# A fused attention and mixture-of-experts kernel: seven expert weight blocks split during the attention, the last head's first half gated two steps sooner, and the written order held through expert 0's first tile

## The chip, the core and the metric

The kernel runs on one core of one Trainium2 chip. The metric is device microseconds (us) of one execution. The engines are named as the profile names them: PE is the matrix engine (PEld its weight loads), DVE the vector engine, ACT the scalar engine, POOL the GpSimd engine, SP the engine whose queue issues most of the DMA transfers. Each engine works through its own instructions in the order in which they stand, and they meet at semaphores.

## What is computed

Two batches of eight heads of attention over 768 positions, in which a query sees only the keys of its own cluster, and then a mixture of eight experts over the 1536 resulting rows, each row sent to its best expert:

```python
mask = q_assign[:, :, :, None] == k_assign[:, :, None, :]
scores = scale * np.matmul(q, k.transpose(0, 1, 3, 2))
scores = np.where(mask, scores, -1000000000.0)
...
attn = attn / (np.sum(attn, axis=-1, keepdims=True) + 1e-09)
return np.matmul(attn, v).astype(np.float32)
...
logits = x @ w_gate
expert_idx = np.argmax(logits, axis=1)
...
h = np.maximum(np.einsum('ecd,edf->ecf', disp, w1), 0.0)
y = np.einsum('ecf,efd->ecd', h, w2)
...
        out[i] = gate_w[i] * y[expert_idx[i], pos[i]]
```

`w1` is 8 x 512 x 1024 and `w2` is 8 x 1024 x 512; an expert keeps its first 384 rows.

## The kernel before

**The attention.** Sixteen heads (index `i` or `h`, 0 to 15; heads 0 to 7 are batch 0) go one after the other. A head has twelve groups `g` (0 to 11). Group `g` is `st_group`: two matmuls (L395, L396) that make a 128 x 384 piece `s` of the scores in PSUM (three buffers), and one ACT instruction (L400) that writes its exponentials to `pf`. What else happens in a group stands in `hooks(i, g)`, called behind each `st_group`; so the order on every engine is written out by hand, and where `held[0]` is set, `keep` pins PE, DVE and ACT instructions to it. The row maxima of a later head are made ahead (`max_tile`, matmuls `m` on PE, reductions `mx` on DVE); they end in head 14's group 2.

At group 2 of head `i` the second half of head `i-1` is finished: `pv_batch` (12 matmuls `o<-pf,v`), sums of the exponentials by matmuls with ones (`sum_strips`, `rsp`), and their copies out of PSUM by ACT (`rs`, `oT`). At groups 5 and 6 the sums are turned (`sum_turn`, `rtp<-cs,rs`, into the one buffer of the PSUM pool `psO` that the values `o` also use) and inverted on DVE (`r`). `out_stage` makes output and gate logits at once (`otp<-rhb,oT`), `out_scale` scales them on DVE into `lg` (logits) and `x`.

**The last head** (15) goes through its keys for the first half of the queries in groups 0 to 5, for the second half in groups 6 to 11. `last_batch` makes values and sums of one half, `sum_turn`, `last_rows` and `last_scale` finish it. Before, the first half starts at group 8, the second after group 11.

**The gate** (`gate`) of three or six row tiles: on DVE the maximum logit (`gmx`), a one-hot row (`goh`) and, from counts that PE makes (`gps`), each row's place (`gsi`); softmax weight by `gex` and `gsm` into `x`. Then POOL scatters each row tile to the table `xd` in DRAM (L649, one indirect DMA a tile, six for the last head). Row tiles of expert 0 beyond the first are read back from `xd` (L806, `row`) and so wait for all six. Expert 0's first tile of 128 rows (tile 0) is full from batch 0 and lies in `row0` since head 10.

**The weights** come in 64 blocks of 512 KB, eight for each expert (0 to 3 of `w1`, 4 to 7 of `w2`). SP loads a block to one of four raw buffers (`wraw`), ACT copies its high part to `ws` (L131, `w_high`), DVE subtracts to get the low part (L137, `w_split`). A raw buffer is free again, and the load of the block four later is issued on SP, when DVE has split it. `W_AT` names the groups in which blocks are split during the attention: before, blocks 0 to 3, as only four `ws` places exist until the attention's tiles (pool `stat`) are freed by `sta.close()` in `moe`. Blocks 4 to 7 are split in expert 0.

**Expert 0** is done tile by tile by `single`: turn the rows (`turn`: four transposes on PE, high part by ACT, low part by DVE: `xha`, `xla` for tile 0, `xhc`, `xlc` for tile 1), two column halves of 12 matmuls each (L878) with ReLU by ACT (`hf`), each turned in the same way (`hha`, `hla`; `hhc`, `hlc`), then 24 matmuls (L848). Between its pieces stand the rest of the last head (`tail`), the row loads, and the splits of expert 0's second four blocks and of expert 1's first four (blocks 8 to 11). Experts 1 to 7 follow, each 448 matmul instructions of L909 and L910 in all seven, with their blocks split on the way.

Of the kernel before, what the change touches and what calls it, by code (L numbers as in the profile page):

```python
# [7 lines left out]
F32 = mybir.dt.float32  # L8
# [15 lines left out]
def kernel(  # L24
# [35 lines left out]
    W_AT = [(13, 8), (14, 2), (14, 8), (15, 2)]  # L60
# [28 lines left out]
    att, sta = ctx.enter_context(ExitStack()), ctx.enter_context(ExitStack())  # L89
    stat = sta.enter_context(tc.tile_pool(name="stat", bufs=1))  # L90
    work = att.enter_context(tc.tile_pool(name="work", bufs=2, side="right"))
    rhb = work.tile([P, H, 2 * OW], F32, name="rhb", bufs=1)
# [368 lines left out]
    def last_batch(h, j):  # L461
        o, ps = psO.tile([P, 512], F32, tag="o", name="o"), psT.tile([P, 512], F32, tag="t", name="rsp")
        pf, a = pt.pop((h, j)), acc.pop((h, j))
        for n in range(TH):
            for c in range(2):
                keep(nc.tensor.matmul(
                    out=o[c * D:(c + 1) * D, 0:HALF],
                    lhsT=vt[h // 2][:, h % 2, 2 * n + c, :],
                    rhs=pf[:, n, c],
                    start=(n == 0),  # L470
                    stop=(n == TH - 1),
                ))
# [23 lines left out]

    def last_scale(h, j):
        b, hh = divmod(h, H)
        r = rt_t[h, "s"]
        tv = oT_t.pop(h)[:, 0:TH * OW].rearrange("p (c o) -> p c o", c=TH)  # L500
        ts = slice(j * TH, (j + 1) * TH)
        lt = work.tile([P, 2, TH, E], F32, tag="lt", name="lt")[:, 0]
        lg = xt[b, "l"][:, ts]
        keep(nc.vector.tensor_tensor(out=lt, in0=tv[:, :, D:OW], in1=r.to_broadcast([P, TH, E]), op=ALU.mult))
        keep(nc.vector.tensor_tensor(out=lg, in0=lg, in1=lt, op=ALU.add))
        keep(nc.vector.tensor_tensor(
            out=xt[b][:, ts, hh * D:(hh + 1) * D], in0=tv[:, :, 0:D], in1=r.to_broadcast([P, TH, D]), op=ALU.mult
# [47 lines left out]
    def gate(b, t0=0, t1=NT):  # L555
# [8 lines left out]
        keep(nc.vector.tensor_reduce(out=mx, in_=lg, axis=AX.X, op=ALU.max))  # L564
        eq = tl("geq")
# [26 lines left out]
        ex = tl("gex")  # L592
        keep(nc.vector.tensor_tensor(out=ex, in0=lg, in1=mx.to_broadcast(sh), op=ALU.subtract))
        keep(nc.scalar.activation(out=ex, in_=ex, func=AF.Exp))

# [78 lines left out]
    row0 = []  # L674

# [4 lines left out]
    def hooks(i, g):  # L680
        even, pi = i % 2 == 0, i // 2
        if g in (3, 9) and 2 <= i < 6:
            zero_fill(2 * (i - 2) + g // 6)
        if i == 3 and g == 0:
# [34 lines left out]
        if i > 0 and g == (G_B0 - 1 if i == NH - 1 else G_OUT) and i != H + 1:  # L719
# [3 lines left out]
        if (i, g) == (H + 1, 5):  # L723
            next(gens["g"])
        if g == G_B1 and i > 0:
# [20 lines left out]
        if g == (G_B0 if i else 2 * NT - 1):  # L746
            if i == NH - 1:
                p_add(i, 0)
                last_batch(i, 0)
            else:  # L750
                pv_batch(i, 0)
                p_add(i, 0)
# [5 lines left out]
            if i == NH - 1:  # L758
                out_scale(i - 1)
# [3 lines left out]
            if not even and i < NH - 3:  # L763
                for _ in gens["c"]:
                    pass
        if (i, g) in W_AT:
# [3 lines left out]
        if g == G_B0 + 1 and 0 < i < NH - 3:  # L770
# [506 lines left out]
```

## Time and profile before

| | us |
|---|---|
| three runs | 469.14, 473.61, 473.76; median 473.61 |
| the profiled execution | 472.46 |
| its span in the trace | 470.3 |
| busy in the span: PE / PEld | 444.9 (95%) / 346.0 (74%) |
| DVE / ACT / POOL | 321.4 (68%) / 272.7 (58%) / 138.5 (29%) |

Times in the rows below are counted from the start of the span. The attention ends at about 265 us; expert 0 ends and expert 1 starts at 299.48 us; the last matmul is over before 465 us. A busy matmul row is as long as the engine holds it, and neighbours overlap, so how long work takes is read from the starts: twelve matmuls of 512 columns start 2.82 us apart from the next piece, 0.235 us each.

### The profile page before, as it was taken

To read this page: it belongs to the slowest core of one execution; us is meant where nothing else is said; L and a number is where in the kernel's file an instruction comes from. 1 tells how busy PE (TensorE), PEld (TensorE's weight loads), DVE (VectorE), ACT (ScalarE), POOL (GpSimd) and SP (SyncE) were. 2 spreads that over 40 slices of the span, in tenths; PEclk is the share of its full clock that TensorE was granted. 3 is DMA by queue.
4 is the path that set the end of the run, shared out by engine and by line. 5 is a ranking of instruction groups with operands and counts; after the bars stand their busy time and mean duration, and the time that the engine had idled before them with its cause. 6 is when DMAs were issued, how large, how long until landed. Compare 5 with 4: busy or idle time off the path is not lost. (4 is left out here: it accounts for less than half of the span.)

```text
span 470.3 us, 8149 instructions
## 1 busy us (share of the span) xinstructions
PE 444.9 (95%) x2832; PEld 346.0 (74%) x2832; DVE 321.4 (68%) x682; ACT 272.7 (58%) x548; POOL 138.5 (29%) x168
## 2 busy tenths in 40 slices
PE   8899999999999989999999978999999999999984
PEld 7764766576666656667755556899999999899963
DVE  6785868678686795787754565587867777687411
ACT  4752655565666555566564624577786868586430
POOL 6793345736334356433000130001010101011010
PEclk9998999999999999999999999999999999999998
DMA  8366449976341514423112058659697878865110
GB/s 281 87 172 214 148 94 344 340 220 231 85 118 35 161 50 147 130 45 88 42 50 91 17 203 307 206 175 289 234 276 252 252 259 238 260 212 204 37 36 18
DMA packets 31223, 78.14 MB, mean 166 GB/s; under 512 B 4678, under 2 KB 5024, under 8 KB 31172
## 3 DMA queue, kind: packets, MB, share of 16 engines
q1 hardware_dynamic: 26340, 61.33, 43.4%
q0 software_dynamic: 4832, 16.15, 8.9%
q8 instruction: 30, 0.49, 0.4%
q14 instruction: 21, 0.17, 0.1%
HBM read 50.46 MB, written 16.76 MB: 143 GB/s over the span
## 5 line engine op out<-in xcount | busy, mean ns | idle before, releaser
L342 DVE TENSOR_REDUCE mx<-m 128x1 f32<-128x384 f32 x192 | 102.5, 553 | 54.1 <-PE m L335 52.2
L400 ACT ACTIVATE pf<-s 128x384 f32<-128x384 f32 x192 | 90.6, 492 | 54.8 <-PE s L396 49.9
L137 DVE TENSOR_TENSOR ws<-wraw,ws 128x1024 fp32r<-128x1024 f32 x64 | 78.1, 1223 | 32.2 <-ACT ws L131 32.0
L395 PE MATMUL s<-W,Y 112*128 112x384 f32 (+1 forms) x192 | 73.7, 384 | 2.0 <-ACT pf L400 2.0
L335 PE MATMUL m<-Y,W 112*128 112x384 f32 (+1 forms) x192 | 68.6, 361 | 5.0 <-DVE mx L342 3.1
L909 PE MATMUL g<-xc,ws 128*128 128x416 f32 x224 | 70.0, 373 | 1.2 <-PEq L1046 0.3
L131 ACT ACTIVATE ws<-wraw 128x1024 fp32r<-128x1024 f32 x64 | 67.0, 1050 | 4.5 <-DMA wraw<-in_w_dram 4.5
L909 PE MATMUL g<-hc,ws 128*128 128x416 f32 x224 | 69.5, 371 | 0.0
L649 POOL DMA_INDIRECT out_dram<-y,row x17 | 18.0, 1057 | 171.5 <-ACT pt L917 110.9
L415 PE MATMUL o<-pf,v 128*64 128x384 f32 x360 | 66.2, 496 | 0.4 <-DVE r L457 0.4
L396 PE MATMUL s<-Qs,Y 97*128 97x384 f32 (+1 forms) x192 | 65.7, 342 | 0.4 <-issue 0.3
L910 PE MATMUL g<-xc,ws 128*128 128x208 f32 x224 | 58.1, 259 | 1.0 <-issue 1.0
L910 PE MATMUL g<-hc,ws 128*128 128x208 f32 x224 | 57.9, 259 | 0.0
L298 POOL TENSOR_TENSOR ql<-qv,W 64x256 fp32r<-64x256 f32 x45 | 39.9, 912 | 51.3 <-ACT W L311 26.2
L298 POOL TENSOR_TENSOR Y<-kv,Y 64x256 fp32r<-64x256 f32 x48 | 41.4, 889 | 43.3 <-ACT Y L316 42.0
L395 PEld LDWEIGHTS s<-W,Y 112*128 112x128 f32 (+1 forms) x192 | 36.5, 190 | 23.2 <-issue 16.6
L917 ACT ACTIVATE pt<-g 128x208 f32<-128x208 f32 x84 | 27.5, 340 | 32.0 <-PE g L910 27.9
L335 PEld LDWEIGHTS m<-Y,W 112*128 112x128 f32 (+1 forms) x192 | 36.5, 191 | 12.9 <-DVE mx L342 8.1
L909 PEld LDWEIGHTS g<-xc,ws 128*128 128x128 f32 x224 | 42.1, 188 | 3.3 <-issue 2.9
L415 PEld LDWEIGHTS o<-pf,v 128*64 128x64 f32 x360 | 23.4, 137 | 28.3 <-issue 24.8
L910 PEld LDWEIGHTS g<-xc,ws 128*128 128x128 f32 x224 | 42.8, 191 | 1.2 <-issue 1.2
L910 PEld LDWEIGHTS g<-hc,ws 128*128 128x128 f32 x224 | 42.7, 191 | 0.0
(206 smaller groups left out, 700.6 us busy)
## 6 DMA issues: line engine op xcount, KB each, us to landing
wraw<-in_w_dram SPq DMA_DIRECT2D x64, 512.0 KB
xd<-z POOLq DMA_DIRECT2D x7, 780.0 KB
row<-xd SPq DMA_DIRECT2D x18, 260.0 KB
qv<-in_qT_dram SPq DMA_DIRECT2D x8, 384.0 KB
kv<-in_kT_dram SPq DMA_DIRECT2D x8, 384.0 KB
v<-in_v_dram SPq DMA_DIRECT2D x8, 384.0 KB
Y<-Y SPq DMA_DIRECT2D x32, 96.0 KB
Qs<-W SPq DMA_DIRECT2D x16, 192.0 KB
```

Of the source, the lines that this page charges most:

```text
L131: keep(nc.scalar.activation(out=w[:, 0], in_=raw[c], func=AF.Copy))
L137: keep(nc.vector.tensor_tensor(out=w[:, 1], in0=t, in1=w[:, 0].bitcast(F32), op=ALU.subtract))
L298: keep(eng.tensor_tensor(out=out[:, cc], in0=a[:, cc], in1=b[:, cc].bitcast(F32), op=ALU.subtract))
L335: keep(nc.tensor.matmul(out=m[:, 0:HALF], lhsT=W[0:KA[h % 2], t * P:(t + 1) * P], rhs=Y1[0:KA[h % 2], j * HALF:(j + 1) * HALF], start=True ...
L342: keep(nc.vector.tensor_reduce(out=mxt[h][:, j, t:t + 1], in_=m[:, 0:HALF], axis=AX.X, op=ALU.max))
L395: keep(nc.tensor.matmul(out=s[:, 0:HALF], lhsT=Y1[0:ka, ks], rhs=W[0:ka, qs], start=True, stop=False))
L396: keep(nc.tensor.matmul(out=s[:, 0:HALF], lhsT=Y0[0:kb, ks], rhs=Qs[0:kb, qs], start=False, stop=True))
L400: keep(nc.scalar.activation(out=pt[h, u][:, slot[0], slot[1]], in_=s[:, 0:HALF], func=AF.Exp, scale=1.0 / float(D) ** 0.5))
L415: keep(nc.tensor.matmul(out=ot[h][j * D:(j + 1) * D, 0:HALF], lhsT=vt[h // 2][:, h % 2, kt, :], rhs=pf[:, n, j], start=(kt == 0), stop=(kt ...
L909: nc.tensor.matmul(out=o, lhsT=w[0], rhs=x.rearrange("p o n -> p (o n)"), start=start, stop=False)
L910: nc.tensor.matmul(out=o[:, 0:RW], lhsT=w[1], rhs=x[:, 0], start=False, stop=stop)
L917: nc.scalar.activation(out=t, in_=o[:, RW:2 * RW], func=AF.Copy)
```

## The change

1. Seven blocks (0 to 6) are split in the attention instead of four: at groups (12,8), (13,2), (13,8), (14,2), (14,8), (15,2), (15,6). The persistent tiles of the heads with an even pair (12 and 13 are the last of them) stand in a pool of their own that is closed at the start of head 14; its room takes the three new `ws` places. The fourth, for block 7, is split behind the last scores. In the groups of `W_AT` the ACT copy is issued ahead of the rest of the group's work.
2. The last head's first half is started at group 6 instead of 8, and its logits and the first half of the gate are done inside groups 10 and 11. The second half's sums come ahead of its values. In `gate` the softmax weight (`gex`, `gsm`) is done sooner, also for batch 0 in head 9.
3. The order stays pinned through the end of the gate: `tail` becomes a generator, three of whose steps stand at named matmuls of expert 0's first tile, and `turn` and the first products are kept in order too.
4. Expert 0 splits only block 7 and then expert 1's blocks 8 to 11.

```diff
-    W_AT = [(13, 8), (14, 2), (14, 8), (15, 2)]
+    W_AT = [(12, 8), (13, 2), (13, 8), (14, 2), (14, 8), (15, 2), (15, 6)]
+    NW = len(W_AT)
...
-        return [[stat.tile([P, S], dt, name=f"{nm}{par}{j}") for j in range(2)] for par in range(2)]
+        return [[stat[j].tile([P, S], dt, name=f"{nm}{par}{j}") for j in range(2)] for par in range(2)]
...
+        if not sums_first:
+            values()
         for q in range(4):
             keep(nc.tensor.matmul(
...
+        if sums_first:
+            values()
...
         keep(nc.vector.tensor_reduce(out=mx, in_=lg, axis=AX.X, op=ALU.max))
+        ex = tl("gex")
+        keep(nc.vector.tensor_tensor(out=ex, in0=lg, in1=mx.to_broadcast(sh), op=ALU.subtract))
+        keep(nc.scalar.activation(out=ex, in_=ex, func=AF.Exp))
         eq = tl("geq")
...
+        sm = tl("gsm", 1)
+        keep(nc.vector.tensor_reduce(out=sm, in_=ex, axis=AX.X, op=ALU.add))
+        keep(nc.vector.tensor_scalar(out=sm, in0=sm, scalar1=1e-9, scalar2=None, op0=ALU.add))
+        keep(nc.vector.reciprocal(out=xt[b][:, t0:t1, DM:DM + 1], in_=sm))
         v, w = tl("gv"), tl("gw")
...
+        if (i, g) == (NH - 2, 0):
+            sta.close()
+            wslot.append(ctx.enter_context(tc.tile_pool(name="wsl", bufs=1, reuse_waits="tile")))
+            for c in range(NA, NW):
+                slots.append(wslot[0].tile([P, 2, 1024], R32, name=f"ws{c}"))
...
-        if i > 0 and g == (G_B0 - 1 if i == NH - 1 else G_OUT) and i != H + 1:
+        if i > 0 and g == (6 if i == NH - 1 else G_OUT) and i != H + 1:
             out_stage(i - 1)
...
+        if (i, g) in W_AT:
+            w_high(W_AT.index((i, g)))
         if g == G_B1 and i > 0:
             pv_batch(i - 1, 1)
...
+        if i == NH - 1:
+            if g == 5:
+                keep(nc.vector.tensor_tensor(out=rhl, in0=rhb[:, H - 1, 0:OW], in1=rhb[:, H - 1, OW:2 * OW], op=ALU.add))
+                p_add(i, 0)
+            if g == 6:
+                last_batch(i, 0)
+                sum_evict(i)
+                pv_evict(i)
+            if g == 7:
+                out_scale(i - 1)
+            if g == 8:
+                sum_turn(i)
+            if g == 9:
+                last_rows(i, 0)
+            if g == 10:
+                last_logits(i, 0)
+                gens["g"] = gate(B - 1, 0, TH)
+                next(gens["g"])
+            if g == 11:
+                next(gens["g"])
+                p_add(i, 1)
+                last_scale(i, 0)
...
-                next(a)
-                tail()
-                for _ in range(FF // 512):
-                    next(a)
-                more_slots(NA)
-                for c in range(NA, 2 * NA):
+                def tail_step():
+                    next(tail, None)
+
+                a = single(0, 0, "a", both, {(0, 0, 0): tail_step, (0, 0, 2): tail_step, (0, 3, 1): tail_step})
+                b = single(0, 1, "b", both)
+                next(a)
+                tail_step()
+                next(a)
+                next(a)
+                more_slots(2 * NA - NW)
+                for c in range(NW, 2 * NA):
                     w_high(c)
...
-                for _ in range(2):
+                for _ in range(2 * NA - NW):
                     w_next()
                 next(a)
-                for _ in range(2):
-                    w_next()
                 next(a)
...
+        def rest():
+            next(gens["g"])
+            yield
+            for _ in gens["g"]:
+                pass
+            last_batch(h, 1, True)
+            sum_evict(h)
+            pv_evict(h)
+            sum_turn(h)
+            yield
+            last_rows(h, 1)
+            last_logits(h, 1)
+            g = gate(B - 1, TH, NT)
+            next(g)
+            next(g)
+            last_scale(h, 1)
+            yield
+            for _ in g:
+                pass
+            counts()
+            held[0] = False
```

**Place 1, ACT, head 14's first groups.** `pf` are exponentials, `rs` and `oT` the copies of head 13's sums and values, `ws` a block's high part. Before:

```order
L400 ACTIVATE pf_2871<-s_2868 128x384
L400 ACTIVATE pf_2871<-s_2876 128x384
L400 ACTIVATE pf_2871<-s_2883 128x384
L443 ACTIVATE rs_2913<-rsp_2904 128x384
L425 ACTIVATE oT_2915<-o_2830 128x384
L131 ACTIVATE ws1_112<-wraw_912 128x1024
L400 ACTIVATE pf_2871<-s_2921 128x384
```

Of the change:

```order
L402 ACTIVATE pf_2882<-s_2879 128x384
L402 ACTIVATE pf_2882<-s_2894 128x384
L402 ACTIVATE pf_2882<-s_2901 128x384
L133 ACTIVATE ws3_117<-wraw_919 128x1024
L445 ACTIVATE rs_2932<-rsp_2923 128x384
L427 ACTIVATE oT_2934<-o_2842 128x384
L402 ACTIVATE pf_2882<-s_2939 128x384
```

The block's copy (block 3 now, block 1 before) moved from behind the two copies to ahead of them; in head 15 the same holds for block 5.

**Place 2, PE and DVE, the end of the last head.** On PE, `s` are score pieces, `rtp<-cs,rs` turned sums, `otp` output and logits, `rtp<-cs,row0` the turned rows of expert 0's first tile, `gps` the gate's counts, `g1` expert 0's products. PE before, from the turn of the first half's sums on:

```order
L450 MATMUL rtp_3100<-cs_75,rs_3092 128x128 x3
L395 MATMUL s_3104<-W11_97,Y111_101 128x384
L396 MATMUL s_3104<-Qs11_105,Y011_109 128x384
L493 MATMUL otp_3112<-rhl_93,oT_3094 128x72 x3
L466 MATMUL o_3131<-pf_3050,v_2641 64x384 x6
L474 MATMUL rsp_3132<-acc_3120,onef_85 32x384 x2
L474 MATMUL rsp_3132<-pf_3050,onef_85 32x384 x2
L878 MATMUL g1_3261<-ws0_111,xha_3186 128x512 x2
L584 LDWEIGHTS trib_81
L584 MATMUL gps_3147<-goh_3129,trib_81 128x48
```

PE of the change, from the same turn on, and then from the last of the counts on:

```order
L452 MATMUL rtp_3114<-cs_75,rs_3098 128x128 x3
L397 MATMUL s_3118<-W11_100,Y111_104 128x384
L398 MATMUL s_3118<-Qs11_108,Y011_112 128x384
L502 MATMUL otp_3126<-rhl_96,oT_3100 128x72 x3
L397 MATMUL s_3130<-W11_100,Y111_104 128x384
L398 MATMUL s_3130<-Qs11_108,Y011_112 128x384
L397 MATMUL s_3147<-W11_100,Y111_104 128x384
L398 MATMUL s_3147<-Qs11_108,Y011_112 128x384
L843 MATMUL rtp_3165<-cs_75,row0_2365 128x128 x4
L602 LDWEIGHTS trib_81
L602 MATMUL gps_3172<-goh_3151,trib_81 128x48
```

```order
L608 MATMUL gps_3172<-gcum_2169,oneb_82 128x48
L481 MATMUL rsp_3205<-acc_3153,onef_85 32x384 x2
L481 MATMUL rsp_3205<-pf_3071,onef_85 32x384 x2
L470 MATMUL o_3204<-pf_3071,v_2644 64x384 x6
L452 MATMUL rtp_3220<-cs_75,rs_3216 128x128 x3
L909 MATMUL g1_3187<-ws0_114,xha_3161 128x512 x2
L502 MATMUL otp_3230<-rhl_96,oT_3218 128x72 x3
```

DVE of the change at that place (`acc` adds the second half's exponentials for `rsp_3205`, `x_2328` are the first half's scaled rows):

```order
L579 TENSOR_REDUCE gmx_3137<-lg_2329 128x3
L581 TENSOR_TENSOR gex_3139<-lg_2329,gmx_3137 128x24
L584 TENSOR_TENSOR geq_3142<-lg_2329,gmx_3137 128x24
L586 TENSOR_TENSOR geq_3142<-geq_3142,cs_75 128x24
L588 TENSOR_REDUCE gm2_3145<-geq_3142 128x3
L591 TENSOR_TENSOR goh_3151<-geq_3142,gm2_3145 128x24
L408 TENSOR_TENSOR acc_3153<-pf_3071 128x768
L518 TENSOR_TENSOR x_2328<-otp_3126,r0_3122 128x3x64
```

The two last score pieces, the turned rows and the first gate's counts moved ahead of the second half's sums; the sums now stand ahead of the values; on DVE, `acc` and `x` stand behind the first gate's one-hot row, where `acc` stood ahead of it. `rsp_3205` waits for `x_2328` (its PSUM buffer was that of `otp_3126`).

**Place 3, SP, the DMA queue from the last maxima on.** `Qs<-mr` are rows of maxima, `row<-xd` the row tiles read back. Before:

```order
L376 DMA Qs11_105<-mr_2931 1x6x128
L120 DMA wraw_2919<-in_w2_dram 128x2x512
L120 DMA wraw_2971<-in_w2_dram 128x2x512
L120 DMA wraw_3029<-in_w2_dram 128x2x512
L806 DMA row_3309<-xd_110 128x520
L806 DMA row_3311<-xd_110 128x520
L806 DMA row_3313<-xd_110 80x520
L806 DMA row_3315<-xd_110 128x520
L806 DMA row_3317<-xd_110 128x520
L120 DMA wraw_3320<-in_w1_dram 128x1024
L120 DMA wraw_3323<-in_w1_dram 128x1024
```

Of the change:

```order
L378 DMA Qs11_108<-mr_2949 1x6x128
L122 DMA wraw_2989<-in_w1_dram 128x1024
L122 DMA wraw_3047<-in_w1_dram 128x1024
L122 DMA wraw_3084<-in_w1_dram 128x1024
L835 DMA row_3325<-xd_113 128x520
L835 DMA row_3327<-xd_113 128x520
L835 DMA row_3329<-xd_113 80x520
L835 DMA row_3331<-xd_113 128x520
L835 DMA row_3333<-xd_113 128x520
L122 DMA wraw_3336<-in_w1_dram 128x1024
```

Loads of blocks 8 to 10 (of expert 1's `w1`) now stand ahead of the row tiles, in the place where those of blocks 5 to 7 stood; only block 11's is behind them, where four were.

## Rows read from the trace of the kernel before

**Rows 1.** Windows by stage: stretch, length, busy us of PE PEld DVE ACT POOL, clock, DMA share, GB/s.
```profile
260.00:280.00 20.00, 16.62 (x102) 11.51 (x102) 13.40 (x51) 9.48 (x18) 6.16 (x6) 1.00 0.26 94
280.00:300.00 20.00, 18.24 (x81) 13.91 (x81) 9.80 (x12) 7.59 (x11) 0.98 (x1) 0.91 0.88 302
300.00:340.00 40.00, 39.85 (x274) 39.37 (x273) 31.78 (x59) 29.52 (x60) 3.17 (x3) 1.00 0.67 216
```

**Rows 2.** Timeline, heads 12 to 15: start, length, engine, line, operation, [idle before <-releaser].
```profile
218.73 1.65 DVE L342 TENSOR_REDUCE mx<-m 128x1 f32<-128x384 f32 x3 [1.09 <-PE m L335]
...
239.40 0.49 ACT L443 ACTIVATE rs<-rsp 128x384 f32<-128x384 f32 x1 [3.32 <-PE rsp L432]
...
252.68 1.06 ACT L131 ACTIVATE ws<-wraw 128x1024 fp32r<-128x1024 f32 x1
...
254.17 0.45 PE L395 MATMUL s<-W,Y 128*128 128x384 f32 x1 [0.78 <-ACT pf L400]
```

**Rows 3.** Timeline of PE, last head: first half's values and turn, second half's turn.
```profile
256.18 2.16 PE L466 MATMUL o<-pf,v 128*64 128x384 f32 x12
...
261.01 0.55 PE L450 MATMUL rtp<-cs,rs 128*128 128x128 f32 x3 [0.98 <-ACT oT L425]
...
267.31 0.49 PE L450 MATMUL rtp<-cs,rs 128*128 128x128 f32 x3
```

**Rows 4.** Timeline of DVE, both gates of the last head.
```profile
263.15 0.95 DVE L406 TENSOR_TENSOR acc<-pf 128x768 f32<-128x768 f32 x1
...
265.34 0.18 DVE L573 TENSOR_TENSOR goh<-geq,gm 128x24 bf16<-128x24 f32 x1
...
269.96 0.18 DVE L573 TENSOR_TENSOR goh<-geq,gm 128x24 bf16<-128x24 f32 x1
...
271.44 0.18 DVE L603 TENSOR_REDUCE gsi<-gv 128x3 int32<-128x24 f32 x1
```

**Rows 5.** Timeline, first and last of six scatters, tile 0's last wait, the row tiles.
```profile
268.35 1.04 POOL L649 DMA_INDIRECT xd<-x,gsi  x1 [48.73 <-issue]
...
274.84 1.20 POOL L649 DMA_INDIRECT xd<-x,gsi  x1 [0.30 <-issue]
275.51 0.60 ACT L885 ACTIVATE hf<-g 128x512 f32<-128x512 f32 x1 [2.24 <-remote]
276.16 0.66 PE L814 MATMUL rtp<-cs,hf 128*128 128x128 f32 x4 [2.34 <-ACT hf L885]
...
277.83 2.23 SPq L806 DMA_DIRECT2D row<-xd  x5
...
280.77 0.63 PE L814 MATMUL rtp<-cs,row 128*128 128x128 f32 x4
```

**Rows 6.** Timeline, tile 1 of expert 0 on PE, its first split, to expert 1's start.
```profile
282.62 0.63 PE L878 MATMUL g<-ws,xhc 128*128 128x512 f32 x2
...
285.15 1.06 ACT L131 ACTIVATE ws<-wraw 128x1024 fp32r<-128x1024 f32 x1 [3.12 <-DMA wraw<-in_w_dram]
285.44 0.60 PE L814 MATMUL rtp<-cs,row 128*128 128x128 f32 x4
...
286.24 1.22 DVE L137 TENSOR_TENSOR ws<-wraw,ws 128x1024 fp32r<-128x1024 f32 x1 [2.67 <-ACT ws L131]
...
290.12 0.74 PE L848 MATMUL g<-ws,hhc 128*128 128x512 f32 x2 [0.86 <-ACT hhc L816]
291.61 0.52 PE L848 MATMUL g<-ws,hlc 128*128 128x512 f32 x1 [0.75 <-DVE hlc L817]
...
295.34 0.64 PE L848 MATMUL g<-ws,hhc 128*128 128x512 f32 x2
...
299.48 0.43 PE L909 MATMUL g<-xc,ws 128*128 128x416 f32 x1
```

**Rows 7.** Windows of 2 us around PE's longest wait and its slow stretch, columns as rows 1.
```profile
274.00:276.00 2.00, 0.00 (x0) 0.00 (x0) 2.00 (x3) 0.49 (x1) 1.70 (x2) 1.00 0.58 223
292.00:294.00 2.00, 2.00 (x9) 1.61 (x7) 0.76 (x1) 0.00 (x0) 0.00 (x0) 0.50 0.63 224
```

More of the change, by code (lines that the diff above doesn't have):

```diff
@@ L459, in sum_scale, with last_batch, values @@
         rt_t[h] = r
-    def last_batch(h, j):
+    def last_batch(h, j, sums_first=False):
         o, ps = psO.tile([P, 512], F32, tag="o", name="o"), psT.tile([P, 512], F32, tag="t", name="rsp")
         pf, a = pt.pop((h, j)), acc.pop((h, j))
[L464 to L472, printed above, removed]
+        def values():
+            for n in range(TH):
+                for c in range(2):
+                    keep(nc.tensor.matmul(
+                        out=o[c * D:(c + 1) * D, 0:HALF],
+                        lhsT=vt[h // 2][:, h % 2, 2 * n + c, :],
+                        rhs=pf[:, n, c],
+                        start=(n == 0),
+                        stop=(n == TH - 1),
+                    ))
+        if not sums_first:
+            values()
         for q in range(4):
@@ L495, in last_rows, with last_logits @@
             ))
+    def last_logits(h, j):
+        b, hh = divmod(h, H)
+        r = rt_t[h, "s"]
+        tv = oT_t[h][:, 0:TH * OW].rearrange("p (c o) -> p c o", c=TH)
+        lt = work.tile([P, 2, TH, E], F32, tag="lt", name="lt")[:, 0]
+        lg = xt[b, "l"][:, j * TH:(j + 1) * TH]
+        keep(nc.vector.tensor_tensor(out=lt, in0=tv[:, :, D:OW], in1=r.to_broadcast([P, TH, E]), op=ALU.mult))
+        keep(nc.vector.tensor_tensor(out=lg, in0=lg, in1=lt, op=ALU.add))
     def last_scale(h, j):
         b, hh = divmod(h, H)
-        r = rt_t[h, "s"]
         tv = oT_t.pop(h)[:, 0:TH * OW].rearrange("p (c o) -> p c o", c=TH)
[L501 to L505, printed above, removed]
         keep(nc.vector.tensor_tensor(
-            out=xt[b][:, ts, hh * D:(hh + 1) * D], in0=tv[:, :, 0:D], in1=r.to_broadcast([P, TH, D]), op=ALU.mult
+            out=xt[b][:, j * TH:(j + 1) * TH, hh * D:(hh + 1) * D],
+            in0=tv[:, :, 0:D],
+            in1=rt_t[h, "s"].to_broadcast([P, TH, D]),
+            op=ALU.mult,
         ))
@@ L765, in hooks @@
                     pass
+        if g == G_B0 + 1 and 0 < i < NH - 3:
+            split(i + 3, 3)
         if (i, g) in W_AT:
@@ L769, in hooks @@
             w_load(c + NA)
[L770 to L780 removed]
+        if i == NH - 1:
+            if g == 5:
+                keep(nc.vector.tensor_tensor(out=rhl, in0=rhb[:, H - 1, 0:OW], in1=rhb[:, H - 1, OW:2 * OW], op=ALU.add))
+                p_add(i, 0)
+            if g == 6:
[16 more added lines that the diff above has]
+                last_scale(i, 0)
     def moe(tail):
[L784 removed]
+        stb.close()
         pools = [ctx.enter_context(tc.tile_pool(name="moe0", bufs=1, reuse_waits="tile"))]
@@ L877, in single @@
                     for n, (a, b) in enumerate(((0, 0), (0, 1), (1, 0))):
-                        nc.tensor.matmul(
+                        if (u, k, n) in between:
+                            between[u, k, n]()
+                        keep(nc.tensor.matmul(
                             out=ps[0:m, 0:UW],
@@ L883, in single @@
                             stop=(k == KD - 1 and n == 2),
-                        )
-                nc.scalar.activation(out=hf[:, u * UW:(u + 1) * UW], in_=ps[0:m, 0:UW], func=AF.Relu)
+                        ))
+                keep(nc.scalar.activation(out=hf[:, u * UW:(u + 1) * UW], in_=ps[0:m, 0:UW], func=AF.Relu))
                 yield
```

64 lines of the change are left out of this document (13 added, 51 removed).

## The prediction, made before the changed kernel was run

> **What bounds the kernel now.** I read the windows by stage first. From 300 us on PE, busy nearly all the time, decides: it lacks 0.15 us in 40 [rows 1], so only time that PE loses ahead of expert 1 can be won. It lacks 3.38 us in 260 to 280 and 1.76 in 280 to 300, where the granted clock is 0.91 besides. The timeline names the losses: waits for ACT in head 15 [rows 2], 0.98 for `oT` [rows 3], 2.34 for `hf` [rows 5], two waits in tile 1 [rows 6]. Behind them stands a chain that PE only follows: gate, six scatters, the row tiles, the turned `row` [rows 4, 5]. In the windows of 2 us the clock is 0.50 after the waits of tile 1 and 1.00 in the long wait of tile 0 [rows 7]. The base of the sum is the profiled execution, 472.46 us (span 470.3), 1.15 below the median 473.61.
>
> **(a) Splits in the attention.** Three more blocks go into heads 12 and 13, where three DVE subtractions and three ACT copies come besides. A copy is 1.06 us [rows 2], a subtraction 1.22 [rows 6]. DVE idles 1.09 before the maxima and ACT 3.32 before `rs` [rows 2]; that covers them, so I cost them at 0 to 0.1. Without that cover PE, which waits for DVE to free the maxima's PSUM buffers, would lose up to 2.4 for two of them. Head 9's earlier softmax weight adds no instruction; DVE's order there is tight, so 0 ± 0.4, taken as 0.
>
> The copies of heads 14 and 15 now stand ahead of `rs` and `oT` (place 1), that is in ACT's idle 3.32. Before, the copy at 252.68 sat in front of the exponentials, and PE waited 0.78 at 254.17 [rows 2]. So the exponentials start about one copy sooner. PE's third piece of head 15 moves 1.0 ahead and the 0.78 goes.
>
> **(b) The last head.** The first half's values started at 256.18 [rows 3]. They move by the 1.0, the 0.78 and two score pieces now behind them (0.35 each): 253.7. Between values and turned sums lie 4.83, of which 0.98 is the wait for `oT` [rows 3]; the copies being earlier, I leave 0.15 of it: turn at 257.7 instead of 261.01. From the second half, where `acc` is not between, turn to one-hot row takes 269.96 − 267.31 = 2.65 [rows 3, 4]; with a score piece of 0.35 ahead of the logits the first half's `goh` is at 260.7, not 265.34.
>
> PE has less to cover this. From the turn to the end of the logits took 1.45 (261.01 to the next batch), then come two pieces (0.7) and the turned `row0` (0.25): out of work at 260.1. It then waits for `goh` (0.18 long) to about 261.0, works 0.15, and waits again, since `acc` (0.95) and `x` stand behind `goh` on DVE and the sums need both: they start at about 262.0. New idle time is 1.75. Sums and values take 2.9 and a copy of `oT` 0.8: second turn at 265.7 instead of 267.31. But seven products of tile 0 (0.235 each, 1.6) done before that turn come later now. PE itself is level: (b) alone gives nothing to PE, it moves the chain.
>
> That chain: behind `goh` DVE does `acc` 0.95, `x` 0.35, `xla` 0.7, the softmax sum 0.6 and four small steps 0.85, so the rows' places are ready at 264.4; with the 0.8 that POOL took after the last of its inputs, the first scatter starts at 265.2 instead of 268.35. The second gate's `goh` is 265.7 + 2.65 + 0.3 for two products ahead of the logits = 268.7, its `gsi` ends 1.66 later (1.48 by [rows 4] and its own length) plus `x`, about 270.5; fourth scatter 271.4. Six scatters start 1.30 apart (6.49 over five intervals [rows 5]): the last starts at 274.0 instead of 274.84. The row loads follow it by 2.99, and a row was turned 2.94 after its load [rows 5]; that is an upper bound, since PE was not waiting for the row alone, and I take 2.5 of 2.2 to 2.94 (2.2 is the length of the five loads' row). `row` is turned at 277.0 + 2.5 = 279.5 (279.2 to 279.9) instead of 280.77: **gain 1.3**.
>
> **(c) Tile 0.** PE's 2.34 wait for `hf` comes from ACT's 2.24, whose releaser ("remote") is none of this kernel's engines [rows 5]. I can't say whether it recurs. Level with before and rid of it, PE is ready for the row at 277.9, with it at about 279.6. Either way this is close to or below the row's 279.5, so a saved wait mostly turns into a wait for the row of up to 1.6: no gain of its own.
>
> **(d) Tile 1.** From 282.62 to 299.48 is 16.86 [rows 6]. Its work is 48 matmuls of 0.235 (282.62 to 285.44, twelve), three turns at 0.36, 0.25 for a short one and 0.3 at the end: 12.9. So 3.9 is lost: 1.1 waiting for `hhc` and 1.0 for `hlc` (the idle times of the rows and what the semaphores take), 1.75 where 291.61 to 295.34 takes 3.73 for seven matmuls and a turn worth 2.0. All follow from ACT, which stood 3.12 in its queue for a raw block [rows 6] with the copies `hhc` behind it. DMA was 0.88 busy there [rows 1]. Place 3 loads blocks 8 to 10 some 25 us sooner; nothing of ACT's queue then waits for a load in tile 1, and `hlc` on DVE stands behind one subtraction at most (about 0.5 of lateness). **Gain 3.4**. Next is late: block 11, behind the row tiles, but its load goes out in a queue that has shed three loads, and expert 1 doesn't need it in its first products.
>
> Of the Trainium skill one rule bears on this: "TensorE: Matmul & The Clock Gate", section "Part 1: The HAM clock gate (the "warmup" mystery)", says that the gate halves PE's clock by how busy PE was lately, and that activity lifts it again. The trace agrees in part: 0.50 stood after tile 1's waits, but 1.00 in a wait as long [rows 7]. By that rule the new idle time of (b) might cost a stretch at half clock; that is rivals B and D.
>
> **Sum.** 1.3 + 3.4 = 4.7: 472.46 − 4.7 = 467.8 on the profiled execution, 468.9 on the median. Expert 1 starts at about 294.8 instead of 299.48.
>
> **Rivals.**
> A. Rows are not late: scatters or loads are quicker, and PE turns the row when ready, 277.9: 1.6 more, 467.3. For it: 2.94 is only an upper bound. Against it: scatters have not become shorter. 0.18.
> B. The clock drops once at the new waits of 260 to 266. Price from the one low stretch seen, 1.75 [rows 6, 7]: 470.6. For it: the 1.75 comes nearly in one piece. Against it: 1.00 after 2.34 idle. 0.17.
> C. The change doesn't do what it says in tile 1: copies and subtractions, though their data are there, still stand ahead of `hhc` and `hlc`, and the waits stay. Then 1.3 + 0.5 is left: 471.8. For it: ACT and DVE keep a block's split between the pieces. Against it: the 3.12 was a wait for a load, not work. 0.11.
> D. Slower: the low clock comes at 262 and holds as long as PE's work has holes, to 272. Some 7.5 us of matmuls (ten, less the 0.8 before the turn and about 1.7 of smaller holes) would take twice as long: 468.9 + 7.5 = 476.4. It is slower than before from 4.7 us of such work on. For it: holes are more frequent there than before, and tile 1 shows the half clock lasting 3.7 us. Against it: clock 1.00 throughout 260 to 280 with 3.38 idle [rows 1]. 0.09.
>
> **How the numbers follow.** My forecast has 0.45 with a range of its own of 468 to 470.5 (rows 279.2 to 279.9, head 9's ± 0.4, a `hlc` wait of 0 to 1). A difference of 1%, 4.7 us, is about what a measurement of this kernel can tell, and the forecast lies at just that edge. Faster by over 1% (below 468.9): half of the forecast and A, 0.23 + 0.18 = 0.41. Within 1%: the other half, B and C, 0.50. Slower: D, 0.09. The range holds A with its scatter of 1.5 below and C with 0.6 above, 465.8 to 472.4, and leaves out D and tails.
>
> **What would show it.** In the changed trace: no wait for `pf` in head 15; values of the first half at about 253.7, its turn at 257.7, `goh` at 260.7 with PE waiting for it and for `x` between 260 and 262; first scatter 265.2, last 274.0; PE waiting up to 1.6 for `row`, turned at 279.5; in tile 1 no ACT wait for a raw block and clock 1.00 from 280 to 300; expert 1 at 294.8. It is wrong if the row comes later than 280, if tile 1 takes over 14.5 us from its first product, if the clock is under 1.00 between 260 and 275, or if heads 12 and 13 grow by more than 0.4.

## The result and the profile after

| | before | of the change |
|---|---|---|
| first comparison, median us | 473.13 (4 runs) | 465.95 (4 runs, 465.39 to 469.2) |
| ratio, 95% interval | | 0.9896 [0.9855, 0.9937] |
| two later comparisons, median us | 470.17 (24 runs), 471.16 (17) | 466.43 (9), 467.53 (12) |
| their ratios | | 0.9919 [0.9890, 0.9949], 0.9924 [0.9891, 0.9957] |
| profiled execution, its span | 472.46, 470.3 | 465.39, 463.2 |

The change makes the kernel faster by about 0.8 to 1.0%. Between the medians of the two larger comparisons that is 3.7 and 3.6 us, where 4.7 was forecast; the 7.2 of the first comparison rests on four runs a side, and its ratio is that of a smaller gain. The windows of the changed kernel, columns as in [rows 1]:

```profile
260.00:280.00 20.00, 17.40 (x99) 12.54 (x100) 9.72 (x39) 5.79 (x11) 5.92 (x6) 1.00 0.42 145
280.00:300.00 20.00, 19.83 (x110) 16.83 (x109) 12.47 (x18) 10.78 (x20) 1.95 (x2) 1.00 0.64 215
300.00:340.00 40.00, 39.70 (x273) 38.97 (x272) 31.65 (x59) 28.93 (x59) 2.18 (x2) 1.00 0.76 242
```

In 280 to 300 PE is busy 19.83 instead of 18.24, at a granted clock of 1.00 instead of 0.91 (the clock has two levels in these rows, 1.00 and 0.50; 0.91 is a mean of both). In 260 to 280 it still lacks 2.60. The timeline of PE, from the last head to expert 1:

```profile
252.43 2.16 PE L470 MATMUL o<-pf,v 128*64 128x384 f32 x12
...
256.42 0.55 PE L452 MATMUL rtp<-cs,rs 128*128 128x128 f32 x3 [0.16 <-ACT oT L427]
...
259.61 0.20 PE L602 MATMUL gps<-goh,trib 128*128 128x48 bf16 x1 [0.49 <-DVE goh L591]
...
260.84 0.52 PE L481 MATMUL rsp<-acc,onef 128*32 128x384 f32 x2 [0.90 <-DVE x L518]
...
264.37 0.55 PE L452 MATMUL rtp<-cs,rs 128*128 128x128 f32 x3 [0.59 <-ACT oT L427]
...
277.74 0.63 PE L843 MATMUL rtp<-cs,row 128*128 128x128 f32 x4 [1.17 <-DMA row<-xd]
...
279.60 0.63 PE L909 MATMUL g<-ws,xhc 128*128 128x512 f32 x2
...
293.02 0.43 PE L940 MATMUL g<-xc,ws 128*128 128x416 f32 x1
```

These answer to [rows 3, 5, 6]. The waits are the forecast ones: for `goh`, for `x`, for `oT`, then for the row, and none in tile 1. The chain beside it (DVE, POOL, SP's queue, ACT) answers to [rows 4, 5]:

```profile
259.37 0.18 DVE L591 TENSOR_TENSOR goh<-geq,gm 128x24 bf16<-128x24 f32 x1
...
263.51 1.03 POOL L663 DMA_INDIRECT xd<-x,gsi  x1 [43.97 <-issue]
...
268.92 0.18 DVE L621 TENSOR_REDUCE gsi<-gv 128x3 int32<-128x24 f32 x1
269.37 0.98 POOL L663 DMA_INDIRECT xd<-x,gsi  x1 [2.27 <-DVE gcu L626]
...
271.94 0.97 POOL L663 DMA_INDIRECT xd<-x,gsi  x1 [0.30 <-issue]
272.05 0.60 ACT L916 ACTIVATE hf<-g 128x512 f32<-128x512 f32 x1 [0.81 <-PE g L909]
274.74 2.22 SPq L835 DMA_DIRECT2D row<-xd  x5
...
279.22 1.07 ACT L133 ACTIVATE ws<-wraw 128x1024 fp32r<-128x1024 f32 x1 [0.22 <-issue]
```

The scatters stand in two groups of three now, as POOL waits for the second gate. ACT's wait ahead of `hf` (2.24 before) is 0.81 and for PE, and its first copy in tile 1 waits for no load.

**One mark for all traces.** By 70 us the traces are up to 4.6 us apart from execution to execution, so the experiments are read from a mark behind that: the start of head 13's second batch of values (235.69 in the trace of before, 234.47 in that of the change). The mark lies between 234.42 and 239.76, and from expert 1's start to the end of the span it takes 169.97 to 170.92, both in no order of kernels. So what sets the kernels apart is read between the mark and expert 1; head 9's clock, below, is the one thing ahead of it. (Each head has two batches. What e2's expectation calls head 14's second is its first, and the 8.74 in e7's ends at head 10's first.) Times in us after the mark:

| kernel | second turn | last scatter | row loads issued | `row` turned | expert 1 starts |
|---|---|---|---|---|---|
| before | 31.62 | 39.15 | 42.14 | 45.08 | 63.79 |
| before again (e8) | 31.61 | 39.15 | 42.06 | 46.41 | 62.43 |
| e1, gate's order | 31.61 | 39.04 | 41.89 | 44.85 | 61.82 |
| e2, copies ahead | 29.72 | 37.25 | 40.26 | 44.60 | 60.44 |
| e5, seven blocks | 29.52 | 38.51 | 41.32 | 44.12 | 59.40 |
| e12, e5 and gate's order | 29.51 | 38.45 | 41.26 | 44.10 | 62.13 |
| e6, change with four blocks | 30.13 | 37.70 | 41.57 | 44.46 | 61.15 |
| change; e7; e9 | 29.90; 29.89; 29.89 | 37.47; 37.46; 37.45 | 40.27; 40.26; 40.25 | 43.27; 43.06; 43.08 | 58.55; 58.33; 58.34 |
| e4; e10, sums first | 28.44; 28.45 | 36.20; 36.24 | 39.01; 39.04 | 42.28; 42.30 | 57.53; 57.55 |

### The profile page after: what moved, and what is told of

Same layout as the page of the kernel before. It is cut to its first block, busy times and chain, and to the rows that moved or that the text cites. A ratio compares the mean times of both kernels' runs of the same rounds, so it can differ in the third digit from the quotient of the medians.

```text
span 463.2 us, 8153 instructions
## 1 busy us (share of the span) xinstructions
PE 442.7 (96%) x2832; PEld 346.7 (75%) x2832; DVE 321.7 (69%) x682; ACT 273.8 (59%) x548; POOL 139.6 (30%) x168
```

## The experiments

**e1: the gate's order alone.**

```diff
         keep(nc.vector.tensor_reduce(out=mx, in_=lg, axis=AX.X, op=ALU.max))
+        ex = tl("gex")
...
+        sm = tl("gsm", 1)
...
         v, w = tl("gv"), tl("gw")
```

> The kernel before with one edit: in `gate` the softmax weight (gex, gsm, x) stands where the change puts it, in head 9 and in the last head. In the changed kernel PE's marks came 0.8 us earlier behind head 9 than ahead of it (from 0.4 to 1.2 earlier than before), where the forecast had 0. Theory 1, the order on DVE in head 9 is the cause: the values of heads 11 to 13 start about 0.8 earlier than in the trace of before, measured against the values of head 7, and PE's two waits for the maxima in 167 to 176 us (0.66 and 1.65 before) fall to about 1.9 together. Theory 2, it is a drift between executions: the two marks keep their distance within 0.2. The last head and tile 1 stay as before in both (the chain at most 0.4 earlier).

Measured: the two waits fell from 2.31 to 1.89, as theory 1 had it, but a third came in the next head. PE's waits for the maxima before, then in e1:

```profile
167.85 0.45 PE L335 MATMUL m<-Y,W 128*128 128x384 f32 x1 [0.66 <-DVE mx L342]
175.93 0.44 PE L335 MATMUL m<-Y,W 128*128 128x384 f32 x1 [1.65 <-DVE mx L342]
```

```profile
166.75 0.45 PE L335 MATMUL m<-Y,W 128*128 128x384 f32 x1 [0.90 <-DVE mx L342]
174.30 0.44 PE L335 MATMUL m<-Y,W 128*128 128x384 f32 x1 [0.99 <-DVE mx L342]
183.38 0.45 PE L335 MATMUL m<-Y,W 112*128 112x384 f32 x1 [0.65 <-DVE mx L342]
```

From head 8's second batch to the mark it took 74.08, before 74.02, in e8 73.93; the change took 73.21 in its first trace and 73.91 in e7, with a third wait of 0.45 there. So the 0.8 of the first trace belonged to that execution: theory 2 for the sum, theory 1 for the two waits. That the largest wait fell from 1.65 to 0.99 matters in another way, below.

**e2: the copies ahead, with four blocks.**

```diff
+        if (i, g) in W_AT:
+            w_high(W_AT.index((i, g)))
         if g == G_B1 and i > 0:
```

> The kernel before with one edit: in the four groups of W_AT the ACT copy of a block is issued ahead of the rest of the group's work. Four blocks, as before. Theory 1, the copy ahead of `rs` is the cause of what came earlier in heads 14 and 15: the values of head 14's second batch start about 0.9 earlier than before (measured from head 13's), the wait of 0.78 for `pf` in head 15 is gone or under 0.2, and the last head's first turn comes 1.5 to 1.9 earlier. Theory 2, the splits that moved to heads 12 and 13 are the cause (fewer copies in heads 14 and 15): less than 0.5 is gained. In tile 1 the waits for raw blocks stay in both, and expert 1's start moves by less than the turn's, 0.5 to 1.8.

Timeline of PE in e2 (head 13's second, head 14's first and head 15's first batch, first turn):

```profile
238.21 2.16 PE L415 MATMUL o<-pf,v 128*64 128x384 f32 x12
...
244.64 2.16 PE L415 MATMUL o<-pf,v 128*64 128x384 f32 x12
...
256.80 2.16 PE L466 MATMUL o<-pf,v 128*64 128x384 f32 x12
...
261.63 0.55 PE L450 MATMUL rtp<-cs,rs 128*128 128x128 f32 x3 [0.67 <-ACT oT L425]
```

Head 14's first batch starts 6.43 after the mark instead of 7.38, the wait for `pf` is gone, and the first turn is 23.42 after the mark instead of 25.32: 1.9 sooner. Theory 1 holds. More: the row loads are issued 40.26 after the mark, exactly where the change has them. Up to the issue of the row loads, the moved copies give all that the chain of gate, scatters and rows gained. The row itself is turned only 4.34 later here, as PE comes to it behind a wait of 2.35 in tile 0 with a clock of 0.50 behind that. Expert 1 starts 3.35 sooner than in the trace of before and 1.99 sooner than in e8, both with a slow clock of their own, and 1.38 sooner than in e1, which has none; the expected 0.5 to 1.8 holds against e1 alone.

**e3: work for PE in tile 1's two waits.**

```diff
+                if dm and n in (0, 2):
+                    dummies(14)
```

> The kernel before, with 14 small matmuls on constants put on PE ahead of tile 1's first product with `hhc` and 14 ahead of the first with `hlc`, that is in its two waits of 0.86 and 0.75. They add work (some 0.8 us each) that nobody uses. Theory 1, the granted clock of 0.50 behind these waits comes from PE being idle in them: with the dummies the clock stays at 1.00 from 291 to 296, and the seven matmuls and the turn behind the wait take about 2.0 instead of 3.73; expert 1 starts 1 to 1.8 earlier measured from tile 1's first product. Theory 2, the clock falls for another reason: 0.50 stays for 3 us or more, and expert 1 starts no earlier.

The clock stayed at 1.00 and the first product to expert 1 took 14.86 instead of 16.86. Both go with theory 1, but e1 and e8 then showed 1.00 in tile 1 without the dummies, so this run does not tell the theories apart.

**e5, e6: the two halves of the change.** e5 is the kernel before with the seven blocks alone, e6 the change with four blocks. In both the copies stand ahead, as in e2; the edit shown is e5's, and e6 takes the same list back:

```diff
-    W_AT = [(13, 8), (14, 2), (14, 8), (15, 2)]
+    W_AT = [(12, 8), (13, 2), (13, 8), (14, 2), (14, 8), (15, 2), (15, 6)]
```

> The kernel before with the change's splits alone: seven blocks in the attention, the copy ahead in the groups of W_AT, only block 7 and blocks 8 to 11 split in expert 0. The last head, the gate and the order behind it stay as before. Marks are measured from head 13's second batch of values (235.69 in the trace of before, 234.47 in that of the change). Theory 1, the forecast's split: tile 1 loses its waits for raw blocks here and takes 13.4 from its first product to expert 1 (16.86 before, of which 1.75 half clock; 13.42 in the change), head 14 and 15 gain 0.9 each, the row is turned 44 to 45 after the mark (45.08 before, 43.27 in the change), and expert 1 starts 59.2 to 60.2 after it (63.79 before, 58.55 in the change). So of the 5.2 between the two, splits carry about 4 and the last head's rework 1.0 to 1.6. Theory 2, the order held through tile 0 and the sooner gate are what frees tile 1: it takes 15 or more here, and expert 1 starts later than 61.

> The changed kernel with only four blocks split in the attention, in the groups of before, and four in expert 0; last head, gate and held order are those of the change. Theory 1, the loads of blocks 8 to 11 behind the row tiles decide tile 1: the row is turned 43 to 44 after head 13's mark as in the change (43.27), ACT waits for a raw block again in tile 1 (3.1 in one wait before), and tile 1 takes 14.5 to 15.5, or 16 to 17 where the clock falls to 0.50 in it; expert 1 starts 60 to 62 after the mark (58.55 in the change). Theory 2, the held order is what frees tile 1: it takes under 14 and expert 1 starts before 59.5.

Rows that decide: PE's row in e5, then ACT's first copy and PE's two waits in tile 1 of e6.

```profile
283.39 0.63 PE L824 MATMUL rtp<-cs,row 128*128 128x128 f32 x4 [3.07 <-DMA row<-xd]
```

```profile
284.56 1.06 ACT L133 ACTIVATE ws<-wraw 128x1024 fp32r<-128x1024 f32 x1 [3.39 <-DMA wraw<-in_w_dram]
```

```profile
288.81 0.73 PE L877 MATMUL g<-ws,hhc 128*128 128x512 f32 x2 [0.42 <-ACT hhc L845]
290.30 0.50 PE L877 MATMUL g<-ws,hlc 128*128 128x512 f32 x1 [0.76 <-DVE hlc L846]
```

Tile 1 takes 13.43 in e5 and 14.84 in e6: theory 1 in both. Only e6's row, turned 44.46 after the mark, is later than the expected 43 to 44; its last scatter took 2.02. The held order does not free tile 1, the loads do. The table gives a short rule. From the issue of the row loads to expert 1 it takes 19.93 and 19.58 with four blocks (e1, e6), and 18.08, 18.28, 18.07 and 18.09 with seven (e5 and the change's three traces). Traces with a slow clock in this stretch are left out: 21.65, 20.37 and 20.18 with four blocks (before, e8, e2) and 20.87 with seven (e12, below). Splits sooner are worth 1.3 to 1.9 behind the issue, copies ahead 1.6 to 1.9 ahead of it (40.26 in e2 against 41.89 to 42.14). In time, e5 had 469.64 against 470.17 (ratio 0.9979 [0.9947, 1.001]), e6 468.8 (0.9969 [0.9938, 0.9999]): each much less than the change's 0.9919 beside them, though e5's trace has all but 1 us of what the change's has behind the mark. It reaches the mark 4.80 later than the change's first trace; 2.93 of that stands by 70 us, and 1.80 comes from head 8's second batch on. Part of this is lost in head 9. Windows of e5 there:

```profile
178.00:180.00 2.00, 1.49 (x8) 1.08 (x9) 1.83 (x6) 0.35 (x1) 1.39 (x3) 0.79 0.34 133
180.00:182.00 2.00, 2.00 (x11) 2.00 (x9) 0.86 (x2) 1.51 (x3) 1.70 (x2) 0.50 0.72 266
182.00:184.00 2.00, 2.00 (x12) 0.83 (x13) 1.56 (x4) 1.33 (x2) 1.39 (x3) 0.85 0.56 181
```

PE's wait of 1.65 in head 9 ended at 178.51, and the clock fell to 0.50 behind it: 9.39 from head 9's first batch to its second instead of the 7.91 of before. That is one execution, and the kernel before has the same wait; so head 9 alone does not explain why e5's median gains no more than 0.53.

**e7, e8: both kernels once more.**

> The changed kernel itself, once more, on the chip of this call. If what its first trace shows is the kernel's and not one execution's: tile 1 takes 13.4 with a clock of 1.00 from 260 to 300, PE's marks from head 13 on repeat within 0.2, and its time is 465 to 467. Two things are held to be of the execution: the stretch from the second batch of head 9 to head 11 (8.74 in the first trace, 9.45 and 9.63 in others with the same order there), and ACT's wait of 2.24 with a releaser outside the kernel ahead of `hf` in tile 0, absent in the first trace. If the wait recurs here, PE takes up to 1.2 of it out of its wait for the row, and expert 1 starts at most 1.1 later measured from head 13.

> The kernel before itself, once more. Theory 1, the clock of 0.50 in tile 1 (1.75 us of the 3.44 that tile 1 gained) belongs to one execution: it is absent here or stands in another place, tile 1 takes about 15.1 and expert 1 starts about 62 after head 13's mark instead of 63.79. Theory 2, it belongs to the kernel's waits: it stands again behind the wait for `hlc`, and tile 1 takes 16.5 to 17.

e7 repeats the change's marks within 0.22, and ACT's wait did not recur. In e8 tile 1 has a clock of 1.00 and takes 14.20; the slow clock stands in tile 0 instead. The wait in tile 0 (timeline of PE) and the windows of e8:

```profile
275.31 0.66 PE L814 MATMUL rtp<-cs,hf 128*128 128x128 f32 x4 [2.34 <-ACT hf L885]
```

```profile
276.00:278.00 2.00, 2.00 (x8) 1.55 (x7) 1.27 (x2) 0.60 (x1) 0.00 (x0) 0.69 0.30 85
278.00:280.00 2.00, 2.00 (x6) 1.61 (x5) 1.68 (x2) 0.00 (x0) 0.00 (x0) 0.50 0.88 302
...
292.00:294.00 2.00, 2.00 (x13) 1.62 (x12) 1.34 (x2) 1.30 (x2) 0.00 (x0) 1.00 0.40 141
```

So theory 1: the place of the slow clock belongs to the execution. The same wait left 1.00 behind it in the first trace [rows 1, 5].

**e4, e10, e9: the sums ahead of the first gate.** The second half's sums and values go ahead of the first gate's counts on PE, `acc` and `x` ahead of the gate on DVE:

```diff
             if g == 10:
                 last_logits(i, 0)
+            if g == 11:
+                p_add(i, 1)
+                last_scale(i, 0)
                 gens["g"] = gate(B - 1, 0, TH)
                 next(gens["g"])
-            if g == 11:
                 next(gens["g"])
-                p_add(i, 1)
-                last_scale(i, 0)
...
         def rest():
+            last_batch(h, 1, True)
             next(gens["g"])
...
-            last_batch(h, 1, True)
```

> The changed kernel with one edit: on DVE the second half's `acc` and the first half's `x` stand ahead of the first gate, and on PE the second half's sums and values ahead of the first gate's counts. Theory 1, PE's 0.49 and 0.90 of waiting at 259 to 261 go into the chain: sums start at about 259.8 instead of 260.84, the second turn 1.0 earlier, the first scatter 0.5 to 1.0 later than 263.5 but the last 0.7 to 1.1 earlier than 271.9; the row is turned 0.7 to 1.1 earlier, expert 1 starts as much earlier. Rival: the first gate, now 1.3 to 2.5 later, becomes the bound (POOL makes the first three scatters before the second three, 1.3 us each): last scatter and expert 1 move by less than 0.3 either way.

> The changed kernel with `acc`, `x`, the second half's sums and values ahead of the first gate, once more and in more rounds. If the 0.8 to 1.0 by which expert 1 started sooner in its first trace (57.53 after head 13's mark) is the kernel's, it recurs within 0.2 and the time is 0.5 to 1 below the change's, 465 to 466; rival: the time is within 0.3 of the change's, because something behind expert 1's start gives it back. ACT's wait of 2.25 ahead of `hf` in tile 0 recurs if it belongs to the six scatters that follow each other without a gap here; if it belongs to one execution it is gone.

> The changed kernel, in as many rounds as the variant it is compared with on this chip. Expected 465.5 to 467, 4 to 5 under the kernel before; expert 1 starts 58.3 to 58.6 after head 13's mark, as in the two traces so far (58.55, 58.33).

The second turn is 1.45 sooner, the six scatters stand together again, the last is 1.26 sooner, and expert 1 starts at 57.53 and 57.55 instead of 58.33 to 58.55: the trace's gain of 0.8 to 1.0 recurs. The time doesn't show it: 466.8 (ratio 0.9902 [0.9863, 0.9942]) in the first comparison, and 467.01 (ratio 0.9895 [0.9851, 0.9939]) beside the change's 467.53 in the second. The medians differ by 0.5 the expected way, which these runs cannot tell from nothing. Both medians lie above what was expected (465 to 466 for e10, 465.5 to 467 for e9), and e9's gain of 3.6 is under the expected 4 to 5. ACT's wait came back in both, here in e10:

```profile
276.43 0.60 ACT L916 ACTIVATE hf<-g 128x512 f32<-128x512 f32 x1 [2.25 <-remote]
```

**e11: a gap between the scatters.**

```diff
+        if b == B - 1 and t0 == TH:
+            for _ in range(2):
+                nc.gpsimd.tensor_copy(gap[1], xt[b][:, t0, DM - 255:DM + 1])
         for t in range(n):
             scatter("xd", xd, si[:, t], xt[b][:, t0 + t, :], (E * ST + 1) * P - 1)
```

> The kernel before with two small copies on POOL between the third and the fourth scatter of the last head (nobody reads what they write). In five traces with six scatters 1.29 apart ACT waited 2.24 to 2.31 ahead of `hf` in tile 0 with a releaser outside the kernel; in five others, where the scatters stood apart in the middle or one of them was long, it did not. Theory 1, the wait hangs on the unbroken row of scatters: with the gap it is under 1.0, and PE's wait of 2.34 in tile 0 goes; the row is turned as much later as the gap is long, 1 to 3 us. Theory 2, it hangs on something else in these programs: it stays at 2.2 to 2.4.

POOL and ACT in e11:

```profile
275.05 0.97 POOL L653 DMA_INDIRECT xd<-x,gsi  x1 [0.30 <-issue]
276.06 0.86 POOL L611 COPY gap<-x 128x256 f32<-128x256 f32 x2
277.25 0.98 POOL L653 DMA_INDIRECT xd<-x,gsi  x1 [0.33 <-issue]
278.53 1.52 POOL L653 DMA_INDIRECT xd<-x,gsi  x1 [0.30 <-issue]
```

```profile
276.70 0.60 ACT L820 ACTIVATE hha<-rtp 128x512 fp32r<-128x512 f32 x1 [2.26 <-PE rtp L818]
277.37 0.60 ACT L889 ACTIVATE hf<-g 128x512 f32<-128x512 f32 x1
```

The spacing at the gap is 0.91 longer than usual (2.20 instead of 1.29), and `hf` follows `hha` with no wait: theory 1. PE's wait of 2.34 in tile 0 shrank to 0.17, but it waited 2.42 for the row instead, which was turned 1.13 later than before. A scatter grew to 1.52, as one did in e5 (1.73), e6 (2.02) and e12 (1.89), where ACT's wait was absent too. Why the row of scatters and ACT's wait go together, no run shows.

The five experiments that ran once took 468.85 (e1), 471.57 (e2), 471.32 (e3), 469.72 (e8) and 475.11 (e11). The kernel before alone spreads over 468.4 to 475.04 in the comparisons beside them, so these times rank nothing, and what the five show stands in their traces.

**e12: the change without the last head's rework.** e5 with the gate's order of e1.

> The kernel before with two parts of the change: the seven blocks with the copies ahead, and the softmax weight done sooner in `gate`. The last head, its first gate at the old place and the free order in expert 0 stay as before. The traces so far give two sums from head 13's mark: the row tiles' loads are issued 42.1 after it in the kernel before, 40.26 with the copies ahead alone and 40.25 to 40.27 in the change; expert 1 starts 19.6 to 20.4 after that issue with four blocks split in the attention, and 18.1 to 18.5 after it with seven. Theory 1, the rework of the last head and the held order bring nothing by themselves: here the loads are issued 40.0 to 40.7 after the mark (up to 1 later where a scatter is long), expert 1 starts 58.2 to 58.9 after it, as in the change (58.33 to 58.55), the clock stays at 1.00 in head 9 as the wait there is 1.0 and not 1.65, and the time is within 1 of the change's, ratio to the kernel before 0.990 to 0.995. Theory 2, the rework carries a good part of the gain, as the forecast had it (1.3 by the chain of gate, scatters and rows): expert 1 starts 59.4 to 60 after the mark, and the ratio is 0.995 or more.

469.28 against 471.58, ratio 0.9938 [0.9905, 0.9971]; the gain of 2.3 is 1.3 to 1.4 less than the change's in its two larger comparisons. The ratio lies in theory 1's span and expert 1's start, 62.13 after the mark, in neither's. The clock stayed at 1.00 in head 9, as expected. PE's row and the windows around it:

```profile
279.18 1.09 PE L823 MATMUL rtp<-cs,row 128*128 128x128 f32 x4 [3.36 <-DMA row<-xd]
```

```profile
276.00:278.00 2.00, 0.00 (x0) 0.00 (x0) 0.00 (x0) 0.00 (x0) 0.00 (x0) 1.00 0.26 40
278.00:280.00 2.00, 0.82 (x5) 0.85 (x5) 0.00 (x0) 0.00 (x0) 0.00 (x0) 0.59 1.01 345
280.00:282.00 2.00, 2.00 (x7) 1.62 (x6) 0.69 (x1) 1.48 (x2) 0.00 (x0) 0.50 1.00 354
```

The loads are issued 41.26 after the mark, with one scatter 0.91 longer than usual in that; without it that would be 40.35, as in the change. So the rework brings the chain nothing beyond that scatter, as theory 1 had it; whether a scatter grows for want of the rework (it did in e5 and e12, and in none of the change's traces), no run separates. But expert 1 starts 2.8 later than 18.1 behind the issue, since the clock fell in a wait of 3.36. With the rework PE waits in four smaller pieces, the longest 1.17, and this is what e5 and e12 lack. Theory 1 misses that.

**The clock over whole runs.** The mean granted clock of each run is on record, and it bears this out. In one set of comparisons it is 0.9898 before (24 runs), 0.9900 in e5 (10), 0.9915 in e6 (10) and 0.9939 in the change (9); in the next 0.9894 before (17) and 0.9927 in the change (12); in the last 0.9889 before (17) and 0.9885 in e12 (12). As an estimate from these, a run's time times what its clock lacks to 1 falls by 1.9 and 1.6 us on average from before to the change, out of gains of 3.9 and 3.7 between the mean times. That is an upper bound, since a low clock costs nothing while PE waits. So up to half of what the change gains is fewer stretches at half clock, and splits and copies without the rework (e5, e12) do not have that part. Why e5's median, at the clock of before, gains only 0.53 while its trace has expert 1 start 2.4 to 3.0 sooner than e1's and e8's, no run shows.

## Why the prediction was right, point by point

- **The number:** 468.9 was forecast, with 465.8 to 472.4 around it. The first comparison measured 465.95, only 0.15 above the lower end, the later ones 466.43 and 467.53. In the later ones the base was too high (470.17 and 471.16 instead of 473.61) by more than the gain was too large; in the first, with four runs a side, the gap between the medians was wider than forecast. That the range held the first median was in part luck.
- **(a) Copies ahead:** 1.0 and 0.78 were forecast, together 1.78; alone in e2 they gave 1.9 at the first turn. The splits in heads 12 and 13 cost nothing: from head 11's first batch to the mark (201.82 to 235.69 before, 200.59 to 234.47 after) it took 33.87 and 33.88. Head 9's order was taken as 0 with ± 0.4 and is about 0 in the sum (e1), apart from the clock: none of the eight traces with it has the slow clock that two of six without it have there.
- **(b) The last head:** from the mark, the marks of the forecast against the trace are 18.0 and 17.96 for the values, 22.0 and 21.95 for the first turn, 25.0 and 24.90 for `goh`, 26.3 and 26.37 for the sums, 30.0 and 29.90 for the second turn. Two terms behind it were mis-sized. The fourth scatter was put 0.9 behind its `gsi`; it started 0.27 behind its end, POOL being in the middle of its work, while the first took the forecast 0.77. The row was put 2.5 behind its load; where PE waits for it, it is 2.80 to 3.00 (3.00 in the change, 2.83 in e9). Together the row came at 43.1 to 43.3 instead of 43.8. The 1.3 in which (b) ends is the copies' doing: e2 issues the row loads at the same 40.26 without the rework.
- **(c) Tile 0:** the wait for `hf` was gone and a wait for the row of 0.97 to 1.17 stood in its place, as forecast (up to 1.6). The 277.9 at which PE was to be ready does not come out of the rows it stands on (280.77 − 2.34 is 278.4), but it came true: PE was free at 276.57, which on the forecast's scale, 1.22 later, is 277.8.
- **(d) Tile 1:** 13.42 against the forecast 13.5. But of the 3.44 gained on the profiled execution 1.74 was the slow clock, which belonged to that execution: e1, with the same waits and a clock of 1.00, took 15.12. So the mechanism, loads that ACT no longer waits for, was right (e5 against e6), and the 3.4 was right by the luck of the execution that it was read from. **The base of the sum was the flaw:** one execution with a slow clock in tile 1. The kernel before in general gives up 3.6 to 3.7 (medians of the larger sets), not 4.7, and lies at 470.2 to 471.6, not 473.61. A slow stretch of some kind does belong to the kernel before on average, as the clocks of whole runs show, but not this one in this place.
- **Rivals:** C fell, the waits of tile 1 are gone. B and D fell: the clock is 1.00 from 260 to 300 in all three traces of the change, behind waits of up to 1.17. The Trainium skill's rule ("TensorE: Matmul & The Clock Gate", section "Part 1: The HAM clock gate (the "warmup" mystery)"), that the clock follows how busy PE was lately, was weighed as a danger to the change; the runs agree with it better the other way round, as a part of the gain (a mean clock of 0.9939 and 0.9927 after, 0.9898 and 0.9894 before). A fell too: the row was late.

## What to carry to other kernels

Where a copy sits in an engine's queue can be worth more than when the work it belongs to is due: copies moved into ACT's idle time gave 1.9 at the first turn, more than the 1.3 that the whole chain behind it was forecast to give. Before a gain is put on a stretch of one trace, look whether that stretch is slow in a second trace of the same kernel; the profiled execution can hold 1.7 us that the next one does not. Where PE must wait, several short waits were cheaper here than one long one of about the same sum (0.49, 0.90, 0.59 and 1.17 in the change, 3.36 in e12), as the clock did not fall behind the short ones in three traces; two short ones close together did cost clock once, in tile 1 of the trace of before.

## What the runs showed of the hardware

- The granted clock fell to 0.50, the lower of its two levels, at a wait of PE in some executions and not in others with the same wait: behind head 9's 1.65 in two of six traces (e2 and e5, 1.2 and 1.5 us), behind tile 0's 2.34 to 2.40 in two of four (e8, e2), in a row wait of 3.36 but not at one of 3.07 or 2.42 (e12; e5, e11). In the seven traces whose longest wait from head 9 to expert 1 was 1.22 or less (the change's three, e4, e10, e1, e6) it never fell there; in tile 1 of the trace of before it fell behind 0.86 and 0.75 close together, and behind nearly the same two waits of e1 (0.71 and 0.76) it did not.
- Six scatters 1.29 apart went with a wait of 2.24 to 2.31 on ACT that no engine of this kernel releases, in six traces (before, e8, e2, e3, e4, e10). The wait was absent where the scatters stood apart in the middle (e6, e11 and the change's three traces; by only 0.15 in e1) or where one took 1.5 to 2.0 instead of 0.98 (e5, e12; also e6 and e11). The cause is open.
